# A fused attention and gated feed-forward block: scaling raw weight blocks on GpSimd, with a reordered start

## Chip, cores and metric

The kernel runs on one core of a Trainium2 chip. The metric is the device time of one execution in microseconds, the median of three runs.

## What is computed

One input `x` of 2048 tokens by 512 is normalised without weights. From it come a sliding-window attention with 32 heads of 16 and a window of 256, and a gated feed forward with 1792 inner columns. The result is `x` plus the product of both.

```python
xn = _layernorm(x)
# s: q, k, v = split(xn @ wqkv); softmax(q k^T / 4 inside the window) v; @ wo
s = _A_ref(xn, A_wqkv, A_wo)                 # H = 32, Dh = 16, W = 256
# B: (silu(xn @ w1) * (xn @ w3)) @ w2
g = _silu(_B_ref(xn, B_w1, B_w3, B_w2))      # F = 1792
return x + s * g
```

## The kernel before

All dense products run in three f16 terms: each f32 operand is scaled by a power of two and split in an upper half (`hi`, the f16 rounding) and a lower half (`lo`, the rest), and hi·hi, lo·hi and hi·lo are summed in PSUM. A split by `split` takes one ScalarE activation (hi, L215) and one VectorE instruction (lo, L216). The feed forward's weights are split by `split_pool`: ScalarE scales the raw block in place in f32 (L224), ScalarE casts it to f16 (L225), and GpSimd subtracts the one from the other in two halves of 256 columns (L221).

The scale of each block comes from its sum of squares. `measure(f)` takes two blocks f and f+1 of 128 feed-forward columns: six raw tiles are squared and summed (`squares`, four on ScalarE at L175, two on VectorE at L177), the sums are cast (`sb`, L187), TensorE multiplies them with ones (`ps`, L200), and a chain of small VectorE instructions makes the powers of two (`al`, `pp`, `pi`, L202 to L207 and L633 to L636). A step or two later the two blocks are split. `measure_down` does the same for the w2 blocks of a group of three or four.

Tokens go in four tiles of 512 (t), heads in four groups of eight (g), feed-forward columns in 14 blocks (f). The raw weights are loaded and split during t = 0 and the split blocks stored to DRAM (`dW1`, `dW2`), from where t = 1 to 3 load them. Raw blocks, split blocks and temporaries share 32 slots of 2 KB per partition (`take`, `give`), so an instruction that fills a slot waits for the last reader of the slot.

TensorE's instructions run in the order in which the Python code issues them; a scheduler orders the other engines. `later(n, f)` puts a function n steps on, and `step()` advances one step. After the start, work is cut into 32 units of attention. `batches` gives a unit's score and value matmuls (L474 for the maxima, L521 for the exponent, L549 for the values), and `spread` puts the dense pieces of six matmuls (L421 projections, L391 values, L682 gate and up, L727 down, L769 output) between those batches.

The start is written out by hand: load x and the first weights, `keep_busy` (filler matmuls that read only ones, L930), layer norm of tile 0 (L319 to L337), transposes on TensorE (L353) into two PSUM tiles `s` of two banks each, the split of the result (L356, L361), projections of group 0 and 1, and `value(0)`, `value(1)`. The softmax's row offsets enter the score product through two extra rows of the operands: `KA[0..2]` hold ones (times 4096) in rows 48, 49, 112 and 113. Before, a small tile `ones` is set by VectorE and six DMAs on SyncE's queue (L980) write it there.

Of the kernel before, what the change touches and what calls it, by code (L numbers as in the profile page):

```python
# [1 line left out]

# [6 lines left out]
F32 = mybir.dt.float32  # L9
BF16 = mybir.dt.bfloat16  # L10
F16 = mybir.dt.float16
# [8 lines left out]
P = 128  # L20
# [22 lines left out]
TERMS = 3  # L43
KR = TERMS * DH
ONE = 2.0**12
VW = DH + 1
VB = 10
SLOTS = 32
# [13 lines left out]
def tile_block(ctx: ExitStack, tc: tile.TileContext, x, wqkv, wo, w1, w3, w2, out):  # L62
# [26 lines left out]
    def take(dtype):  # L89
        slot = free.pop(0)  # L90
        made = fpool.tile([P, 512 if dtype == F32 else 1024], dtype, name=slot, tag=slot, bufs=1)
        held[id(made)] = slot, made
        return made

    def give(*tiles):
        for made in tiles:
            free.append(held.pop(id(made))[0])
# [14 lines left out]
    def later(n, f):  # L112
        made_so_far[0] += 1
        queue.append((now[0] + n, made_so_far[0], f))
# [93 lines left out]

    def scaled(a, by, name):
        t = const.tile([P, 1], F32, name=name)  # L210
        nc.vector.tensor_scalar(t, a, by, None, op0=ALU.mult)
        return t

    def split(hi, lo, raw, s):
# [6 lines left out]
            op(out[:, c], a[:, c], b[:, c])  # L221

    def split_pool(hi, lo, raw, s):
        nc.scalar.activation(raw, raw, AF.Copy, scale=s)  # L224
        nc.scalar.copy(hi, raw)  # L225
        halves(nc.gpsimd.tensor_sub, lo, raw, hi)


# [77 lines left out]
    def prepare(t):  # L306

        mv = lnpool.tile([P, 4, 2], F32, name="mv")
        rs = lnpool.tile([P, 4], F32, name="rs")
        xts = {}  # L310
        pair = {}

        def load(b):
            xts[b] = take(F32)
            (nc.scalar if t == 0 and b % 2 else nc.sync).dma_start(xts[b], x[t * TW + b * P:t * TW + (b + 1) * P, :])

        def stats(b):
            st = lnpool.tile([P, nc.vector.BN_STATS_DIM], F32, name="st")
            nc.vector.bn_stats(st, xts[b])  # L319
            nc.vector.bn_aggr(mv[:, b, :], st)  # L320

        def rstd(b0, b1):
            ve = lnpool.tile([P, b1 - b0], F32, name="ve")
            nc.vector.tensor_scalar(ve, mv[:, b0:b1, 1], 1e-5, None, op0=ALU.add)

            r0 = lnpool.tile([P, b1 - b0], F32, name="r0")
            nc.vector.tensor_scalar(r0.bitcast(I32), ve.bitcast(I32), 1, None, op0=ALU.logical_shift_right)
            nc.vector.tensor_scalar(r0.bitcast(I32), r0.bitcast(I32), -1.0, float(0x5F3759DF), op0=ALU.mult, op1=ALU.add)
            sq = lnpool.tile([P, b1 - b0], F32, name="sq")
            for i in range(3):  # L330
                nc.vector.tensor_mul(sq, r0, r0)
                nc.vector.scalar_tensor_tensor(sq, sq, -0.5, ve, op0=ALU.mult, op1=ALU.mult)
                nc.vector.scalar_tensor_tensor(r0, sq, 1.5, r0, op0=ALU.add, op1=ALU.mult)
            nc.vector.tensor_scalar(rs[:, b0:b1], r0, XS, None, op0=ALU.mult)

        def centre(b):
            lasts["centre"] = nc.vector.tensor_scalar(xts[b], xts[b], mv[:, b, 0:1], rs[:, b:b + 1],  # L337
                                                      op0=ALU.subtract, op1=ALU.mult)

        def turn(b):  # L340
            if t not in X:
                X[t] = xpool.tile([P, NC, TW], F16, name="XH"), xpool.tile([P, NC, TW], F16, name="XL")
            xh, xl = X[t]
            c = slice(b * P, (b + 1) * P)
            if t:
                pt = psm.tile([P, NC, P], F32, name="mm", tag="mm")
            else:

                if b % 2 == 0:
                    pair["s"] = pss.tile([P, 2, 512], F32, name="s")  # L350
                pt = pair["s"][:, b % 2, :].rearrange("p (k q) -> p k q", q=P)
            for k in range(NC):
                nc.tensor.transpose(pt[:, k, :], xts[b][:, k * P:(k + 1) * P], identf)  # L353
            give(xts.pop(b))
            with urgent():
                lasts["xh"] = nc.scalar.copy(xh[:, :, c], pt)  # L356

            def rest():
                turned[t] = turned.get(t, 0) + 1
                with urgent():  # L360
                    lasts["x"] = nc.vector.tensor_sub(xl[:, :, c], pt, xh[:, :, c])  # L361
            later(1, rest)
        return load, stats, rstd, centre, turn
# [82 lines left out]
    def fetch(t, g):  # L446
        QA[t, g] = qa = qpool.tile([P, 4, TW], F16, name="qa")
        ka = keys(t, g)
        c0 = 0 if t else 2 * P
        for dst, d in ((ka[:, :, c0:], dK[g][:, :, t * TW - 2 * P + c0:(t + 1) * TW]),  # L450
                       (qa, dQ[g][:, :, t * TW:(t + 1) * TW])):
            for r in range(2):
                nc.sync.dma_start(dst[64 * r:64 * r + KR],
                                  d[64 * r:64 * r + 64].rearrange("(a d) i t -> (d i) a t", d=DH))
# [348 lines left out]
    def feed_forward():  # L803

        pieces = []
        late = []
        for t in range(NT):
            for f in range(FB):
                if t == 0:
                    if f % 2:  # L810
                        pieces += [(0, lambda f=f: load(0, f)) for f in range(f + 3, min(f + 5, FB))]
                    elif f + 2 < FB:
                        pieces.append((0, lambda f=f + 2: measure(f, 1)))
                    pieces += [(0, lambda k=k: measure_down(k)) for k, (_, f1) in enumerate(GROUPS) if f == f1 - 1]
                else:
                    if f == 0:
                        pieces += [(0, lambda t=t, f=f: load(t, f)) for f in range(2)]
                    if f + 2 < FB:
                        pieces.append((0, lambda t=t, f=f + 2: load(t, f)))
                if f == FB - 4 and t + 2 < NT:  # L820
                    first, second = prepare_beside(t + 2)
                    pieces += first
                pieces += [(6, q) for q in gate_up(t, f)]
                pieces += late
                late = []
                for k, (f0, f1) in enumerate(GROUPS):
                    if f == f1 - 1:
                        late = [q for b in range(4) for q in down(t, k, b)]
            if t + 2 < NT:
                pieces += second  # L830
        return pieces + late
# [48 lines left out]
    def spread(made, dense):  # L880

        whole = sum(c for c, _ in dense) + sum(c for c, _ in made)
        dense = list(dense)
        at = 0
        for k, (cost, batch) in enumerate(made):
            batch()
            step()
            at += cost
            while dense and (at < whole * (k + 1) / len(made) or dense[0][0] == 0):
                c, piece = dense.pop(0)  # L890
                at += c
                piece()
                if c:
                    step()
        run(dense)

    def run(dense):
        for c, piece in dense:
            piece()
            if c:  # L900
                step()
# [3 lines left out]
    qk = [weights_qk(g) for g in range(NG)]  # L905
    wv = weights("wv", wqkv[:, 2 * D:3 * D])
    wout = weights("wo", wo)
    ones = take(F16)
    nc.vector.memset(ones[0:4, 0:KW], ONE)
    for b in range(4):  # L910
        load0(b)
    qk[0][0]()
    qk[1][0]()
    wv[0]()
# [7 lines left out]
    for b in range(VB):  # L922
        nc.gpsimd.memset(V[:, b, 0:H * VW].rearrange("p (h w) -> p h w", w=VW)[:, :, DH:VW], 1.0)
    nc.gpsimd.memset(V[:, :, H * VW:], 0.0)


    def keep_busy(n):
        ps = psm.tile([P, 4, P], F32, name="ps", tag="mm")
        for _ in range(n):
            nc.tensor.matmul(ps, onesb, onesb.unsqueeze(1).to_broadcast([P, 4, P]), start=True, stop=True)  # L930

    keep_busy(22)
    for b in range(4):
        stats0(b)
    qk[0][1]()
    qk[0][2]()
    keep_busy(9)
    rstd0(0, 4)
    for b in range(4):
        centre0(b)  # L940
# [10 lines left out]
        flush()  # L951
    with tc.issue_after(lasts["hi"].ins), tc.issue_after(lasts["x"].ins):
        qk[1][1]()
        wv[1]()
    keep_busy(4)


    k00, q00 = (project(0, 0, k, ((0,), (1,), (2,))) for k in (1, 0))
    run([k00[0], q00[0], k00[1], q00[1]])
    qk[1][2]()  # L960
    qk[1][3]()
    with tc.issue_after(lasts["hi"].ins):
        run([k00[2], q00[2]])
# [10 lines left out]
        measure(0)  # L974
    run(project(0, 1, 0))
    later(1, lambda: fetch(0, 1))
    run(value(0))
    for r in range(3):
        for q in range(2):
            nc.sync.dma_start(KA[r][64 * q + KR:64 * q + KR + 2], ones[2 * q:2 * q + 2, 0:KW].unsqueeze(1).to_broadcast([2, 4, KW]))  # L980
    give(ones)
    qk[2][1]()
    run(value(1))
    qk[2][2]()
# [91 lines left out]
```

## Time and profile before

| what | value |
|---|---|
| runs | 885.81, 888.51, 890.38 us; median 888.51 |
| profiled execution | 888.54 us, span 886.8 us |
| TensorE, weight load (PEld) | busy 847.0 us (96%), 375.9 us (42%) |
| VectorE (DVE) | 623.7 us (70%) |
| ScalarE (ACT) | 441.1 us (50%) |
| GpSimd (POOL) | 193.4 us (22%) |
| moved by DMA | 110.51 MB, 125 GB/s |

All times inside the execution are in microseconds from the start of the span. A row of the timeline gives start, duration, engine, line, operation, output and input tiles, and in brackets the idle time of the engine before it with what ended it. A name such as PEq or SPq is the engine's sequencer, where DMAs are issued. A group row gives count, total busy time and the mean in nanoseconds.

### The profile page before, as it was taken

The numbers are of one execution on the slowest core, as the hardware profiler recorded it, in microseconds if no ns is written. First come the engines' busy times: TensorE is split into PE (matmuls) and PEld (weight loads), VectorE is DVE, ScalarE is ACT, GpSimd is POOL, SyncE is SP. The second block draws the span as 40 slices with busy tenths as digits, with TensorE's granted clock in tenths as the row PEclk, the third lists the DMA queues.
The fourth block names the chain that finished last, engine by engine and source line by source line (L and its number), as shares of the span: only waits on it lengthen the run. The fifth ranks groups of instructions, "written<-read, shape, count | busy, mean of one in ns | idle before, by whom it ended". The sixth has DMA issues, their size and how long they took to land.

```text
span 886.8 us, 20443 instructions
## 1 busy us (share of the span) xinstructions
PE 847.0 (96%) x7814; PEld 375.9 (42%) x7814; DVE 623.7 (70%) x1833; ACT 441.1 (50%) x649; POOL 193.4 (22%) x308
## 2 busy tenths in 40 slices
PE   7968898999999999999999999999999999999997
PEld 3323344344444444444444444444444444444443
DVE  7676866797678667768767776777767786666435
ACT  4777767673435544443444444444444444444521
POOL 1236226352111202111111112120211103131211
PEclk9989999999999999999999999999999999999999
DMA  9864525646543343452445333533443353332201
GB/s 294 222 221 157 154 80 170 182 147 192 149 133 95 103 118 111 108 150 73 125 121 128 100 89 103 160 102 101 117 126 79 87 140 111 99 110 84 75 9 60
DMA packets 95133, 110.51 MB, mean 125 GB/s; under 512 B 16972, under 2 KB 60348, under 8 KB 95036
## 3 DMA queue, kind: packets, MB, share of 16 engines
q1 hardware_dynamic: 94748, 108.69, 42.9%
q8 instruction: 61, 1.00, 0.5%
q10 hardware_dynamic: 288, 0.52, 0.2%
q14 instruction: 36, 0.29, 0.1%
HBM read 76.28 MB, written 28.57 MB: 118 GB/s over the span
## 4 chain that ended last, share of the span: by engine, by line
PE 70%; DVE 9%; ACT 6%; DMA 5%; issue 5%; POOL 3%; SPq 1%; POOLq 0%; DVEq 0%; ACTq 0%
PE mm L682 25%; PE mm L727 14%; PE po L549 8%; PE mm L421 6%; PE s L521 6%; PE s L474 4%; PE mm L769 4%; PE mm L391 3%; DVE junk L479 3%; POOL slot L221 2%; DMA slot<-in_A_x_dram 1%; ACT pt L539 1%; DMA slot<-in_B_w_dram 1%; ACT sqa L175 1%; ACT slot L225 1%
## 5 line engine op out<-in xcount | busy, mean ns | idle before, releaser
L539 ACT ACTIVATE pt<-s,es 128x1024 f32<-128x1024 f32 (+1 forms) x184 | 200.9, 1094 | 224.0 <-DVE s L535 115.3
L682 PE MATMUL mm<-XH,slot 128*128 128x512 f16 x896 | 269.2, 382 | 1.6 <-DVE XL L361 1.2
L221 POOL TENSOR_TENSOR slot<-slot,slot 128x256 f16<-128x256 f32 (+1 forms) x220 | 146.9, 694 | 537.5 <-ACT slot L706 410.3
L479 DVE CUSTOM_DVE_ANT_0 junk<-s,MW 128x320 bf16<-128x320 f32 x448 | 218.0, 487 | 24.0 <-PE s L474 13.7
L682 PEld LDWEIGHTS <-slot 128*128 128x128 f16 x1344 | 121.7, 98 | 161.7 <-issue 29.4
L682 PE MATMUL mm<-XL,slot 128*128 128x512 f16 x448 | 170.5, 381 | 0.0
L727 PE MATMUL mm<-slot,slot 128*128 128x512 f16 x672 | 160.7, 383 | 1.7 <-DVE XL L361 1.4
L535 DVE TENSOR_TENSOR s<-s,M 128x512 f32<-128x512 f32 x128 | 89.0, 696 | 72.4 <-PE s L521 67.6
L549 PE MATMUL po<-pt,V 128*32 128x128 f32 (+1 forms) x1920 | 98.3, 330 | 0.0
L727 PEld LDWEIGHTS <-slot 128*128 128x128 f16 x672 | 61.1, 98 | 82.6 <-issue 16.3
L474 PE MATMUL s<-KA,qa 48*64 48x320 f16 (+2 forms) x1024 | 73.6, 298 | 12.6 <-DVE M L479 8.5
L530 DVE TENSOR_TENSOR s<-s,M 128x1024 f32<-128x1024 f32 x56 | 68.8, 1228 | 19.6 <-PE s L521 15.9
L521 PE MATMUL s<-qa,KA 50*64 50x128 f16 (+1 forms) x1920 | 74.2, 251 | 5.6 <-ACT pt L539 2.8
L521 PEld LDWEIGHTS <-KA 50*64 50x64 f16 x1920 | 33.7, 105 | 80.2 <-issue 47.4
L697 DVE SCALAR_TENSOR_TENSOR slot<-slot,mm 128x512 f32<-128x512 f32 x56 | 38.4, 685 | 41.3 <-ACT slot L693 41.1
L706 ACT CAST slot<-slot 128x512 f16<-128x512 f32 x56 | 34.5, 616 | 53.2 <-DVE slot L702 53.1
L549 PEld LDWEIGHTS po<-pt,V 128*32 128x32 f32 x1920 | 49.8, 109 | 24.8 <-issue 12.0
L693 ACT ACTIVATE slot<-mm,sgs 128x512 f32<-128x512 f32 x56 | 38.2, 682 | 27.5 <-PE mm L682 23.8
L702 DVE SCALAR_TENSOR_TENSOR slot<-mm,slot 128x512 f32<-128x512 f32 x56 | 38.6, 688 | 18.6 <-PE mm L682 18.5
L221 POOL TENSOR_TENSOR on<-on,rb 128x256 f32<-128x256 f32 x32 | 22.6, 727 | 127.9 <-DMA qa<-dm 82.9
L743 DVE SCALAR_TENSOR_TENSOR slot<-mm,dsc,slot 128x512 f32<-128x512 f32 x48 | 35.9, 749 | 20.5 <-PE mm L727 20.4
L421 PE MATMUL mm<-XH,whi 128*128 128x512 f16 x128 | 47.1, 381 | 1.2 <-ACT whi L215 1.2
(122 smaller groups left out, 828.1 us busy)
## 6 DMA issues: line engine op xcount, KB each, us to landing
slot<-dW SPq DMA_DIRECT2D x126, 256.0 KB
slot<-in_B_w_dram SPq DMA_DIRECT2D x42, 256.0 KB
dW<-slot SPq DMA_DIRECT2D x42, 256.0 KB
slot<-in_A_x_dram SPq DMA_DIRECT2D x30, 256.0 KB
KA<-dK SPq DMA_DIRECT2D x24, 288.0 KB
qa<-dQ SPq DMA_DIRECT2D x32, 192.0 KB
dK<-slot SPq DMA_DIRECT2D x16, 256.0 KB
dQ<-slot SPq DMA_DIRECT2D x16, 256.0 KB
```

The costliest lines, as they stand in the source:

```text
L221: op(out[:, c], a[:, c], b[:, c])
L421: nc.tensor.matmul(cell["pp"], a[:, k, c, :], b[:, c, :], start=(c, i) == parts[0][0], stop=(c, i) == parts[-1][-1])
L474: nc.tensor.matmul(s[64 * c:64 * c + 64, r, :n], qa[rows, 2 * p + a, ii * P + 64 * c:ii * P + 64 * c + 64], ka[rows, 2 * p + a, e - n:e], ...
L479: nc.vector.tensor_tensor_reduce(out=junk[:, :n], in0=s[:, r, :n], in1=mask, scale=1.0, scalar=NEG, op0=ALU.add, op1=ALU.max, accum_out=M[ ...
L521: nc.tensor.matmul(s[h:h + 64, r, o:o + w * P], ka[rows, 2 * p + a, (j + 2) * P + h:(j + 2) * P + h + 64], qa[rows, 2 * p + a, q * P:(q + ...
L530: nc.vector.tensor_add(sv, sv, m.unsqueeze(1).to_broadcast([P, 4, 2, P]))
L535: nc.vector.tensor_add(sv[:, :, b, :], sv[:, :, b, :], M2[:, k:k + 1, :].to_broadcast([P, 4, P]))
L539: nc.scalar.activation(pt[:, :, 0:n], s.rearrange("p r (a q) -> p (r a) q", a=2)[:, :, 0:n], AF.Exp, scale=es)
L549: nc.tensor.matmul(cell["po"][32 * i:32 * i + 32, q * P:(q + w) * P], V[:, (4 * t + j) % VB, h * VW:h * VW + 32], pt[:, i, o:o + w * P], s ...
L682: nc.tensor.matmul(cell[k], w[:, (a * NC + c) * P:(a * NC + c + 1) * P], b[:, c, :], start=c == 0 and i == 0, stop=c == NC - 1 and i == 2)
L702: nc.vector.scalar_tensor_tensor(sg, cell[1], 0.5 * HS / (WS * XS)**2, sg, op0=ALU.mult, op1=ALU.mult)
L727: nc.tensor.matmul(ps, hh[:, a * TW + b * P:a * TW + (b + 1) * P], w[:, c * D:(c + 1) * D], start=f == f0 and i == 0, stop=f == f1 - 1 and ...
```

## The change

Six things are changed together.

- `split_pool`: ScalarE writes hi straight from the raw block with the scale; GpSimd multiplies the raw block by the scale in place, in two halves, and then subtracts as before.
- The rows of ones: no DMA any more. VectorE sets all of `KA[0]`, ScalarE all of `KA[1]` from a tile of ones, GpSimd all of `KA[2]`.
- Transposes of tile 0: each of the four has its own PSUM tile (two `s`, one `po`, one `mm`).
- The fillers: 27, 5 and 4 where there were 22, 9 and 4.
- `wv`'s squares come after the scale of `qk[1]`, whose product stands four matmuls earlier; `measure(2, 1)` is called before `value(0)`, and not at block 0 of the feed forward.
- `spread`: after each batch, dense pieces are issued as long as at least half of the next one lies within the share of dense work due by then; before, as long as that share was not yet reached.

```diff
+TWO_ONES = struct.unpack("f", struct.pack("ee", ONE, ONE))[0]
...
     def split_pool(hi, lo, raw, s):
-        nc.scalar.activation(raw, raw, AF.Copy, scale=s)
-        nc.scalar.copy(hi, raw)
+        nc.scalar.activation(hi, raw, AF.Copy, scale=s)
+        for c in (slice(0, 256), slice(256, 512)):
+            nc.gpsimd.tensor_scalar(raw[:, c], raw[:, c], s, None, op0=ALU.mult)
         halves(nc.gpsimd.tensor_sub, lo, raw, hi)
...
-            if t:
+            if t or b == 3:
                 pt = psm.tile([P, NC, P], F32, name="mm", tag="mm")
+            elif b == 2:
+                pt = pso.tile([P, TW], F32, name="po").rearrange("p (k q) -> p k q", q=P)
             else:
-                if b % 2 == 0:
-                    pair["s"] = pss.tile([P, 2, 512], F32, name="s")
-                pt = pair["s"][:, b % 2, :].rearrange("p (k q) -> p k q", q=P)
+                pt = pss.tile([P, 2, 512], F32, name="s")[:, 0, :].rearrange("p (k q) -> p k q", q=P)
...
-                    elif f + 2 < FB:
+                    elif 0 < f < FB - 2:
                         pieces.append((0, lambda f=f + 2: measure(f, 1)))
...
-            while dense and (at < whole * (k + 1) / len(made) or dense[0][0] == 0):
+            while dense and (at + dense[0][0] / 2 <= whole * (k + 1) / len(made) or dense[0][0] == 0):
...
-    ones = take(F16)
-    nc.vector.memset(ones[0:4, 0:KW], ONE)
     for b in range(4):
         load0(b)
+    nc.vector.memset(KA[0].rearrange("p a c -> p (a c)").bitcast(F32), TWO_ONES)
+    nc.scalar.activation(KA[1].rearrange("p a (b c) -> p (a b) c", c=P), onesb.unsqueeze(1).to_broadcast([P, 24, P]),
+                         AF.Copy, scale=ONE)
...
+    for a in range(4):
+        nc.gpsimd.memset(KA[2][:, a, :].bitcast(F32), TWO_ONES)
...
-    keep_busy(22)
+    keep_busy(27)
...
-    keep_busy(9)
+    keep_busy(5)
...
         qk[1][1]()
-        wv[1]()
     keep_busy(4)
     k00, q00 = (project(0, 0, k, ((0,), (1,), (2,))) for k in (1, 0))
-    run([k00[0], q00[0], k00[1], q00[1]])
+    run([k00[0], q00[0], k00[1]])
     qk[1][2]()
+    with tc.issue_after(lasts["scale"].ins):
+        wv[1]()
+    run([q00[1]])
     qk[1][3]()
...
     later(1, lambda: fetch(0, 1))
+    measure(2, 1)
     run(value(0))
-    for r in range(3):
-        for q in range(2):
-            nc.sync.dma_start(KA[r][64 * q + KR:64 * q + KR + 2], ones[2 * q:2 * q + 2, 0:KW].unsqueeze(1).to_broadcast([2, 4, KW]))
-    give(ones)
```

More of the change, by code (lines that the diff above doesn't have):

```diff
@@ L1 @@
+import struct
 from contextlib import ExitStack, nullcontext
```

3 lines of the change are left out of this document (1 added, 2 removed).

## The prediction

> **What bounds the kernel now.** I read the page first, then busy time by stage, then TensorE's waits, then the timeline of the stage with the longest wait.
>
> ```profile
> span 886.8 us, 20443 instructions
> PE 847.0 (96%) x7814; PEld 375.9 (42%) x7814; DVE 623.7 (70%) x1833; ACT 441.1 (50%) x649; POOL 193.4 (22%) x308
> ```
> ```profile
> 0.00:60.00 60.00, 47.83 (x247) 20.91 (x248) 42.02 (x162) 38.33 (x84) 14.22 (x40) 0.94 0.83 239
> 60.00:200.00 140.00, 125.84 (x1090) 55.02 (x1089) 105.07 (x377) 98.94 (x175) 62.34 (x96) 0.99 0.51 155
> 200.00:860.00 660.00, 651.30 (x6371) 289.62 (x6370) 463.48 (x1274) 299.54 (x384) 112.08 (x168) 1.00 0.40 111
> 860.00:886.80 26.80, 22.06 (x111) 10.35 (x109) 13.10 (x21) 4.33 (x7) 4.78 (x8) 0.98 0.16 50
> ```
> ```profile
> PE s L474 <- DVE M L479: 8.5, 10, 2.0
> PE ps L200 <- DVE sb L187: 7.4, 3, 5.3
> ```
>
> The columns of the second fence are stretch, length, then busy time of PE, PEld, DVE, ACT and POOL, then TensorE's granted clock, DMA share and GB/s. TensorE is the bound: busy 847.0 of 886.8 us. It idles 60 - 47.83 = 12.2 us in the first 60 us, 14.2 us from 60 to 200, 8.7 us in the next 660 and 4.7 at the end. The matmuls that compute stay the same, so the change can only move idle time, filler matmuls, and time at a lower clock; all three lie mostly in front. After 200 us hardly anything is left to win. The third fence (engine line, who it waited for: total, times, longest) shows that one wait of 5.3 us stands out.
>
> ```profile
> 45.67 0.60 PE L682 MATMUL mm<-XH,slot 128*128 128x512 f16 x2
> ```
> ```profile
> 46.32 0.59 PE L682 MATMUL mm<-XH,slot 128*128 128x512 f16 x2
> ```
> ```profile
> 48.41 0.63 ACT L175 ACTIVATE sqa<-slot 128x512 bf16<-128x512 f32 x1
> ```
> ```profile
> 52.22 0.17 DVE L187 CAST sb<-ssq 128x6 bf16<-128x6 f32 x1 [1.97 <-ACT sqa L175]
> 52.45 0.17 PE L200 MATMUL ps<-sb,onesb 128*128 128x6 bf16 x1 [5.32 <-DVE sb L187]
> 52.55 0.75 PE L474 MATMUL s<-KA,qa 48*64 48x320 f16 x8
> ```
> ```profile
> 53.23 1.04 PE L682 MATMUL mm<-XH,slot 128*128 128x512 f16 x2
> ```
> ```profile
> 57.31 0.31 PE L474 MATMUL s<-KA,qa 48*64 48x128 f16 x8
> ```
>
> This is `measure(2)`: TensorE's order is written by hand, so its small L200 product blocks all behind it until the squares of blocks 2 and 3 are summed, and ScalarE starts those only at 48.41. After the stall the same pair of matmuls that took 0.59 us takes 1.04: the clock has fallen.
>
> **The change part by part.**
>
> *measure(2) is moved ahead of `value(0)`.* In the built kernel its L200 now stands some 60 matmuls earlier, before `value(2)`, and the score matmuls follow block 0's feed forward directly. Gone: 5.3 us of stall. Gone too: the slow stretch behind it. From 52.55 to 57.31 there are 8 score matmuls and 12 of L682 in 4.76 us; at the early pace (a pair and its single from 45.67 to 46.32, three matmuls in 0.65 us, so 12 in 2.6) plus 0.75 they take 3.3. That is 1.4 us. The granted clock of 0.94 over the first 60 us holds this stretch. The Trainium skill ("TensorE: Matmul & The Clock Gate", Part 1) says that an idle window of about 3.4 us halves TensorE's clock until a busy window has passed; the pair's 1.04 against 0.59 us agrees. Together 5.3 + 1.4 = 6.7 us.
>
> *What the moved squares now stand in front of.* This is the debit, and it hangs on ScalarE's queue.
>
> ```profile
> 12.55 1.09 PE L353 MATMUL s<-identf,slot 128*128 128x128 f32 x8 [0.68 <-ACT XH L356]
> 14.37 0.66 PE L353 MATMUL s<-identf,slot 128*128 128x128 f32 x4 [0.73 <-ACT XH L356]
> 21.39 0.15 DVE L211 TENSOR_SCALAR sw<-invqk 128x1 f32<-128x1 f32 x1
> ```
> ```profile
> 22.35 1.04 PE L421 MATMUL mm<-XH,whi 128*128 128x512 f16 x4 [1.24 <-ACT whi L215]
> 25.62 0.15 DVE L211 TENSOR_SCALAR swwv<-invwv 128x1 f32<-128x1 f32 x1
> ```
> ```profile
> L177 DVE CUSTOM_DVE_ANT_0 sqd<-slot 128x512 bf16<-128x512 f32 x20 | 14.2, 725 | 5.8 <-DMA slot<-in_B_w_dram 5.6
> ```
> ```profile
> 30.95 0.57 ACT L430 ACTIVATE slot<-mm 128x512 f16<-128x512 f32 x1
> 31.30 0.17 PE L200 MATMUL ps<-sb,onesb 128*128 128x6 bf16 x1 [0.60 <-DVE sb L187]
> 32.00 0.62 ACT L175 ACTIVATE sqa<-slot 128x512 bf16<-128x512 f32 x1
> 34.31 0.19 PE L200 MATMUL ps<-sb,onesb 128*128 128x1 bf16 x2
> 40.31 0.59 PE L682 MATMUL mm<-XH,slot 128*128 128x512 f16 x2
> ```
>
> First the start. One filler matmul more in all stands where TensorE waits anyway: 0. With a PSUM bank for each transpose the waits of 0.68 and 0.73 go, 1.4 us. With `wv`'s squares behind the scale of `qk[1]` the wait of 1.24 goes. But what is late next is `swwv` (25.62). The scale of `qk[1]` (21.39) comes to about 18.3: 1.4 earlier by the start, and some 1.7 by squares that stood before it. From there VectorE's new order has nine instructions on 128x512 before `swwv` (four squares at 0.725, the two cuts and three L434, which I price alike at 0.7) and a few small ones: 18.3 + 6.4 + 0.2 = 24.9. So it is 0.7 to 0.9 us earlier, not 2.6, and TensorE then waits about 1 us for `wvh`. So ScalarE reaches L430 (30.95) at about 30.1 and TensorE its L200 (31.30) at 30.4.
>
> From there ScalarE's new order is: L430 and the evacuation of V (30.95 to 32.00, 1.05 us), four squares of `measure(2)` and two of `qk[2]`, at 0.61 us each. That is 30.1 + 1.05 + 3.7 = 34.9. TensorE's L200 for `qk[2]` (34.31, without a wait) needs the last of them: it moves to 35.1, 0.8 later than before, after a wait of about 1.7. A further 0.4 goes to the product of `measure(2)` itself and the bank it frees. Block 0's first matmul goes from 40.31 to about 41.5. Net of the whole start: +1.2 us. The bounds are -2.6 (the start's gain kept whole) and +2.5 (the waits of 1 to 1.7 us also drop the clock once more).
>
> *The rows of ones.*
>
> ```profile
> 1.55 0.70 DVE L909 MEMSET slot<- 4x768 f16 x1
> ```
> ```profile
> 6.77 0.63 ACT L175 ACTIVATE sqa<-slot 128x512 bf16<-128x512 f32 x1 [3.82 <-DMA slot<-in_A_wqkv_dram]
> ```
> ```profile
> L539 ACT ACTIVATE pt<-s,es 128x1024 f32<-128x1024 f32 x176 | 195.5, 1112 | 218.2 <-DVE s L535 109.5 <-DVE s L530 107.7 <-ACT slot L706 0.3
> ```
> ```profile
> L539 ACT ACTIVATE pt<-s,es 128x512 f32<-128x512 f32 x8 | 5.4, 681 | 5.8 <-DVE s L535 5.8
> ```
> ```profile
> 35.64 2.64 SPq L980 DMA_DIRECT2D KA<-slot  x4
> ```
>
> VectorE's memset grows from 768 to 1536 elements, so from 0.70 to about 1.4, and ends at 3.0, when it waits for x. ScalarE fills 3072 elements before its first square; at 0.43 us for 512 more (0.681 for 512, 1.112 for 1024) that is some 2.8 us, inside the 3.82 that it waits. GpSimd's four memsets lie where it has nothing to do. SyncE loses six issues, 2.64 us of them in front of the next loads; but behind those stands the store of block 0's weights, which waits for GpSimd, so I give no credit. Nothing here reaches TensorE: 0. If the cover of VectorE or ScalarE failed it would cost what sticks out, under 1 us.
>
> *The split of the raw blocks.*
>
> ```profile
> L225 ACT CAST slot<-slot 128x512 f16<-128x512 f32 x42 | 24.6, 612 | 4.7 <-POOL slot L221 3.0 <-DMA dK<-slot 1.7
> ```
> ```profile
> L215 ACT ACTIVATE whi<-slot,sw 128x512 f16<-128x512 f32 x8 | 5.5, 717 | 5.5 <-DVE sw L211 5.5
> ```
> ```profile
> L221 POOL TENSOR_TENSOR slot<-slot,slot 128x256 f16<-128x256 f32 x196 | 130.0, 690 | 494.5 <-ACT slot L706 410.3 <-ACT slot L225 82.3 <-issue 1.4
> ```
> ```profile
> masks.py:199 POOL TENSOR_SCALAR_AFFINE_SELECT identf<-identf 128x128 f32<-128x128 f32 x1 | 0.3, 293 | 0.0
> ```
> ```profile
> 82.98 0.39 PE L682 MATMUL mm<-XH,slot 128*128 128x512 f16 x1 [0.36 <-POOL slot L221]
> ```
>
> ScalarE loses 42 casts, 24.6 us; the scaling that is left writes f16, as L215's does, at 0.717 each. GpSimd gains 84 multiplies. No such instruction is in the trace: the one-input select on half the elements (0.293) and the two-input subtraction of the same size (0.690) are the ends. I take 0.45, nearer the one-input row, with part of it fixed and the elements doubled: 38 us, range 25 to 58. By the Trainium skill ("GPSIMD Engine Reference", § 3.1) a tight one-input loop takes about 1.8 cycles an element, an estimate of 0.38 us for 256, so 32 us. GpSimd is busy 62 of 140 us between 60 and 200; with three quarters of the new work there it comes to about 90. The lower half is ready after one activation, two multiplies and two subtractions, 0.7 + 0.9 + 1.4 = 3.0 us; before, two activations and the same subtractions, 2.7 us. The one place where TensorE waited for it (0.36) stays about that. On SyncE's in-order queue the loads of block 6 now stand behind the stores of blocks 1 and 2, which wait for GpSimd's halves; the squares that need those loads come some 20 us later, so 0. ScalarE's relief and GpSimd's load I set against each other: 0, from -3 to +4.
>
> *Piece spreading.* `spread` now rounds to the nearest piece rather than up. In the built order the runs of dense matmuls between attention batches shift by one piece; before 78 runs of 6, 66 of 12, 44 of 18, after 72, 72, 41. No work is added; at stake are the waits left after 60 us, 14.2 + 8.7 = 23 us. I take 0, plus or minus 4.
>
> *Sum.* -6.7 + 1.2 = -5.5. The profiled execution took 888.54 us with a span of 886.8, 1.7 outside it; the runs' median is 888.51, so both give the same: 883.0 us, -0.6%. What a measurement of this kernel can tell from no change is about 0.5%, 4.4 us.
>
> **The rivals.**
>
> *The front gains whole and the later waits shrink too (chance 0.20).* The start keeps its 2.6 us, and of the 23 us some 4 go, ScalarE being 24.6 us lighter. For: TensorE also waits for ScalarE between 60 and 200. Against: VectorE's waits are larger. 888.5 - 6.7 - 2.6 - 4 = 875.
>
> *The stall only moves (0.17).* The waits of 1 and 1.7 us around 30 to 35 grow to a long one, since six squares stand in a row before `qk[2]`'s product, and the clock falls there: +2.5 and 1.4 more than my sum. 888.5 - 5.5 + 3.9 = 887. For: ScalarE's queue stands between all the steps there. Against: 1 and 1.7 us are well under the 5.3 that the slow matmuls followed.
>
> *GpSimd takes VectorE's port, and VectorE's lateness reaches TensorE: slower (0.18).*
>
> ```profile
> 53.06 0.17 DVE L206 TENSOR_SCALAR pp<-al 128x6 f32<-128x6 f32 x1
> ```
> ```profile
> 77.97 1.30 POOL L221 TENSOR_TENSOR slot<-slot,slot 128x256 f16<-128x256 f32 x2 [1.57 <-ACT slot L706]
> 78.70 0.59 DVE L206 TENSOR_SCALAR pp<-al 128x6 f32<-128x6 f32 x1
> ```
>
> The same 6-element instruction takes 0.17 us with GpSimd idle and 0.59 during one of its subtractions. If each of the 84 multiplies holds up VectorE by 0.42 us, that is 35 us; where 40% of it reaches TensorE through the scores' maxima (the 8.5 us line above), 14 us: 888.5 - 5.5 + 14 = 897. Against: the slow row reads and writes SBUF alone, while the maxima and mask additions read PSUM. It decides once more than 10 us reach TensorE. The Trainium skill has this rule ("GPSIMD Engine Reference", § 8): GpSimd shares its SBUF interfaces with VectorE, and § 4.1 prefers VectorE for elementwise work. By that rule the time is this rival's; the rows agree on a small instruction, and no run here shows a multiply.
>
> **How the numbers follow.** The forecast has 0.45 and its own range 878 to 888. Chances: forecast 0.45, of which 0.33 lies below 884.1 and 0.12 within 0.5%; first rival 0.20, faster; second 0.17, of which 0.02 faster and 0.15 same; third 0.18, slower. So faster 0.55, same 0.27, slower 0.18. The range for 8 in 10 takes in the forecast, the second rival and most of the first, and the lower part of the third: 874 to 892.
>
> **What would show each step.** Right: no wait above 2.1 us before an L200 behind block 0, a granted clock near 1.0 from 50 to 60, block 0's first matmul at 41 to 42, the L474 now at 57.31 at about 52; GpSimd's busy time at 218 to 253 and ScalarE's at about 419. Wrong: a wait of over 2.1 us before `qk[2]`'s product, TensorE's idle time from 60 to 200 well off 14, L206-like rows of 0.6 us in most blocks, or multiplies above 0.69 us.

## The result and the profile after

The changed kernel takes 936.35 us (median of four runs, 935.12 to 938.62) against 887.32 us (885.81 to 890.38) for the kernel before: a ratio of 1.0566, 95% interval 1.0542 to 1.0590. That is slower by 49 us. The forecast was 883.0 us, range 874 to 892. The profiled execution took 938.62 us with a span of 936.8.

From the page of the changed kernel, the span and the busy times:

```profile
span 936.8 us, 20492 instructions
...
PE 866.8 (93%) x7815; PEld 382.0 (41%) x7815; DVE 632.4 (68%) x1833; ACT 423.1 (45%) x608; POOL 270.0 (29%) x396
```

Busy time by stage, in the columns of the prediction's second fence:

```profile
0.00:60.00 60.00, 51.42 (x274) 22.76 (x275) 43.97 (x170) 39.24 (x83) 30.29 (x61) 1.00 0.87 242
60.00:200.00 140.00, 101.30 (x712) 41.63 (x711) 79.00 (x258) 57.55 (x100) 88.97 (x119) 0.81 0.34 105
200.00:860.00 660.00, 642.06 (x6280) 283.92 (x6278) 474.03 (x1351) 301.81 (x395) 138.69 (x200) 0.99 0.42 117
```

The first 60 us became better: TensorE is busy 51.42 us where it was 47.83, at a clock of 1.00 where it was 0.94. The next 140 us lost it all. TensorE is idle 140 - 101.3 = 38.7 us there (14.2 before) and runs at a granted clock of 0.81 (0.99). Over the whole span idle time went from 886.8 - 847.0 = 39.8 to 936.8 - 866.8 = 70.0 us, 30 more; busy time grew by 20 us for practically the same matmuls. So of the 50 us, three fifths are waiting and two fifths are matmuls that ran slower. Five waits of TensorE between 60 and 200 us last 6.6, 3.8, 4.1, 7.1 and 8.3 us (they end at 97.72, 117.08, 127.19, 163.16 and 196.09), 29.9 of the 38.7; in the 4 us behind each of them the granted clock is 0.50. Before, no wait of TensorE in this stage was longer than 2.0 us.

GpSimd's groups by line, operation and shape:

```profile
L224 POOL TENSOR_TENSOR slot<-slot,slot 128x256 f16<-128x256 f32 x196 | 128.3, 677 | 399.1 <-ACT slot L709 399.1
L229 POOL TENSOR_SCALAR slot<-slot,pi 128x256 f32<-128x256 f32 x56 | 53.1, 959 | 42.1 <-ACT slot L227 42.1
L229 POOL TENSOR_SCALAR slot<-slot,sw 128x256 f32<-128x256 f32 x28 | 25.9, 937 | 28.6 <-ACT slot L227 28.6
```

L229 is the new multiply, L224 the subtraction (L221 before). A multiply takes 0.94 to 0.96 us, not 0.45, and more than a subtraction that reads two inputs. One block occupies GpSimd for 2 x 0.95 + 2 x 0.68 = 3.26 us where it took 2 x 0.69 = 1.38.

How that reaches TensorE is seen in the list of waits (who, for whom: total, times, longest):

```profile
PE s L477 <- DVE M L482: 26.2, 9, 8.2
...
ACT slot L227 <- POOL slot L224: 23.6, 5, 7.7
ACT sqa L178 <- DMA slot<-in_B_w_dram: 23.5, 8, 8.6
...
ACT O L596 <- POOL on L224: 17.6, 6, 10.3
...
PE s L524 <- ACT pt L542: 10.6, 7, 6.3
...
PEld L685 <- POOL slot L229: 7.3, 1, 7.3
PE mm L685 <- DVE slot L700: 7.1, 1, 7.1
```

The three waits of ScalarE in the kernel before:

```profile
ACT O L593 <- POOL on L221: 13.4, 8, 2.8
...
ACT sqa L175 <- DMA slot<-in_B_w_dram: 3.3, 3, 1.9
...
ACT slot L225 <- POOL slot L221: 3.0, 4, 1.5
```

TensorE's matmuls wait for VectorE's maxima (L482) and for ScalarE's exponents (L542), hardly ever for GpSimd itself. One weight load (PEld) is put down to GpSimd with 7.3 us; it starts 0.01 us after the matmul in front of it, and that matmul's wait is the last line of the list. But ScalarE waits for GpSimd, and other engines wait for ScalarE. The longest wait of TensorE, in the timeline; the rows between the lines shown are left out:

```profile
189.31 1.83 POOL L229 TENSOR_SCALAR slot<-slot,pi 128x256 f32<-128x256 f32 x2
191.09 1.30 POOL L224 TENSOR_TENSOR slot<-slot,slot 128x256 f16<-128x256 f32 x2
192.34 1.41 POOL L224 TENSOR_TENSOR on<-on,rb 128x256 f32<-128x256 f32 x2
193.79 0.62 ACT L596 CAST O<-on 128x512 f16<-128x512 f32 x1 [10.28 <-POOL on L224]
194.31 0.59 ACT L433 ACTIVATE slot<-mm 128x512 f16<-128x512 f32 x1
...
194.94 0.69 DVE L437 SCALAR_TENSOR_TENSOR slot<-mm,slot 128x512 f16<-128x512 f32 x1 [8.64 <-ACT slot L433]
...
195.54 0.48 DVE L482 CUSTOM_DVE_ANT_0 junk<-s,MW 128x320 bf16<-128x320 f32 x1
...
196.09 0.32 PE L477 MATMUL s<-KA,qa 48*64 48x128 f16 x4 [8.25 <-DVE M L482]
```

GpSimd works through weight blocks without a pause until 192.34 and only then normalises the attention's output (`on`). ScalarE's next instruction, the cast of it, has stood 10.28 us at the head of its queue. Behind the cast stands L433, behind that VectorE's L437 (8.64 us), behind that the maxima, and TensorE has waited 8.25 us. No one on that chain needs a weight block. The maker of the delay is GpSimd's order, and the engine that TensorE's row names is three links further.

A second way goes through SyncE's queue (SPq), to the wait of 6.6 us:

```profile
90.33 3.38 SPq L690 DMA_DIRECT2D dW<-slot  x2
...
92.06 1.29 POOL L224 TENSOR_TENSOR slot<-slot,slot 128x256 f16<-128x256 f32 x2
...
93.80 0.38 SPq L318 DMA_DIRECT2D slot<-in_A_x_dram  x1
...
96.64 0.69 DVE L322 BATCH_NORM_STATS2 st<-slot 128x6 f32<-128x512 f32 x1 [7.31 <-DMA slot<-in_A_x_dram]
...
97.72 0.43 PE L477 MATMUL s<-KA,qa 48*64 48x256 f16 x4 [6.59 <-DVE M L482]
```

The store of a split block (L690) stands at the head of SyncE's queue until GpSimd has made the lower half at 93.35; the load of x behind it goes out at 93.80, VectorE's statistics stand 7.31 us for it, and TensorE 6.59.

A third way goes through the slots, to the wait of 7.1 us:

```profile
158.21 0.72 ACT L227 ACTIVATE slot<-slot,sw 128x512 f16<-128x512 f32 x1 [6.18 <-POOL slot L224]
...
161.71 0.69 ACT L696 ACTIVATE slot<-mm,sgs 128x512 f32<-128x512 f32 x1 [2.17 <-POOL slot L224]
...
162.43 0.69 DVE L700 SCALAR_TENSOR_TENSOR slot<-slot,mm 128x512 f32<-128x512 f32 x1 [3.69 <-ACT slot L696]
...
163.16 1.01 PE L685 MATMUL mm<-XH,slot 128*128 128x512 f16 x2 [7.06 <-DVE slot L700]
```

ScalarE stands twice until a subtraction on GpSimd lets it write a slot, VectorE stands for ScalarE, and TensorE for the PSUM bank that VectorE reads. How the loss divides among the three ways is not measured.

### The profile page after: what moved, and what is told of

Same layout as the page of the kernel before. It is cut to its first block, busy times and chain, and to the rows that moved or that the text cites. A ratio compares the mean times of both kernels' runs of the same rounds, so it can differ in the third digit from the quotient of the medians.

```text
span 936.8 us, 20492 instructions
## 1 busy us (share of the span) xinstructions
PE 866.8 (93%) x7815; PEld 382.0 (41%) x7815; DVE 632.4 (68%) x1833; ACT 423.1 (45%) x608; POOL 270.0 (29%) x396
## 4 chain that ended last, share of the span: by engine, by line
PE 67%; POOL 12%; issue 8%; DVE 6%; ACT 4%; DMA 3%; SPq 0%; POOLq 0%; ACTq 0%; DVEq 0%
PE mm L685 23%; PE mm L730 12%; PE po L552 8%; POOL slot L229 6%; PE mm L424 5%; PE s L524 5%; POOL slot L224 5%; PE mm L772 4%; PE mm L394 4%; PE s L477 3%; DVE s L533 2%; DVE junk L482 2%; ACT pt L542 1%; PE ps L937 1%; DMA slot<-in_B_w_dram 1%
## 5 line engine op out<-in xcount | busy, mean ns | idle before, releaser
L542 ACT ACTIVATE pt<-s,es 128x1024 f32<-128x1024 f32 (+1 forms) x184 | 200.8, 1093 | 209.2 <-DVE s L533 104.3
L685 PE MATMUL mm<-XH,slot 128*128 128x512 f16 x896 | 275.7, 390 | 9.1 <-DVE slot L700 7.1
L224 POOL TENSOR_TENSOR slot<-slot,slot 128x256 f16<-128x256 f32 (+1 forms) x220 | 145.2, 682 | 441.1 <-ACT slot L709 399.1
L482 DVE CUSTOM_DVE_ANT_0 junk<-s,MW 128x320 bf16<-128x320 f32 x448 | 217.9, 486 | 31.8 <-PE s L477 21.0
L685 PEld LDWEIGHTS <-slot 128*128 128x128 f16 x1344 | 124.1, 100 | 175.2 <-issue 38.3
L685 PE MATMUL mm<-XL,slot 128*128 128x512 f16 x448 | 173.7, 388 | 0.0
L730 PE MATMUL mm<-slot,slot 128*128 128x512 f16 x672 | 164.8, 391 | 0.3
L730 PEld LDWEIGHTS <-slot 128*128 128x128 f16 x672 | 62.3, 100 | 83.2 <-issue 18.0
L229 POOL TENSOR_SCALAR slot<-slot,pi 128x256 f32<-128x256 f32 x56 | 53.1, 959 | 42.1 <-ACT slot L227 42.1
L224 POOL TENSOR_TENSOR on<-on,rb 128x256 f32<-128x256 f32 x32 | 22.6, 727 | 127.7 <-DMA qa<-dm 65.4
L477 PEld LDWEIGHTS <-qa 48*64 48x64 f16 x1024 | 29.0, 107 | 57.4 <-DVE M L482 30.4
```

The costliest lines, as they stand in the source:

```text
L229: nc.gpsimd.tensor_scalar(raw[:, c], raw[:, c], s, None, op0=ALU.mult)
L477: nc.tensor.matmul(s[64 * c:64 * c + 64, r, :n], qa[rows, 2 * p + a, ii * P + 64 * c:ii * P + 64 * c + 64], ka[rows, 2 * p + a, e - n:e], ...
L482: nc.vector.tensor_tensor_reduce(out=junk[:, :n], in0=s[:, r, :n], in1=mask, scale=1.0, scalar=NEG, op0=ALU.add, op1=ALU.max, accum_out=M[ ...
L542: nc.scalar.activation(pt[:, :, 0:n], s.rearrange("p r (a q) -> p (r a) q", a=2)[:, :, 0:n], AF.Exp, scale=es)
L685: nc.tensor.matmul(cell[k], w[:, (a * NC + c) * P:(a * NC + c + 1) * P], b[:, c, :], start=c == 0 and i == 0, stop=c == NC - 1 and i == 2)
L730: nc.tensor.matmul(ps, hh[:, a * TW + b * P:a * TW + (b + 1) * P], w[:, c * D:(c + 1) * D], start=f == f0 and i == 0, stop=f == f1 - 1 and ...
```

## The experiments

Three theories of the loss stood at first. Theory 1: the multiplies make GpSimd the slow stage while t = 0, and queues that run in order stall behind it. Theory 2: each multiply takes a port from VectorE, and VectorE is late. Theory 3: the loss is in the start or the spreading. The kernel before ran beside every group, at medians of 886.5 to 887.9 us, so comparisons across groups go by ratio to it; differences of ratios are turned into us with 887.3.

### Which part loses

`rest_only`: the changed kernel with the old split.

```diff
-        nc.scalar.activation(hi, raw, AF.Copy, scale=s)
-        for c in (slice(0, 256), slice(256, 512)):
-            nc.gpsimd.tensor_scalar(raw[:, c], raw[:, c], s, None, op0=ALU.mult)
+        nc.scalar.activation(raw, raw, AF.Copy, scale=s)
+        nc.scalar.copy(hi, raw)
         halves(nc.gpsimd.tensor_sub, lo, raw, hi)
```

> The changed kernel with the old split of the raw blocks (two ScalarE instructions, GpSimd only subtracts); start, measure(2), rows of ones and spreading stay changed. Theory 1 (the multiplies make GpSimd the slow stage of the weight preparation while t = 0, and engines that run in order stall behind it): all the loss is gone and the front's gain is left, 888.5 - 5.5 = 883 us, 880 to 886, GpSimd busy about 196 us, no wait above 3 us on TensorE between 60 and 200 us. Theory 2 (the multiplies slow VectorE through a shared port): the same 883. Theory 3 (the new order of the start or of the dense pieces loses): over 900 us.

Measured: 883.13 us, ratio 0.9959 (0.9944 to 0.9974). `split_only` is the kernel before with the opposite edit, the new split alone:

> The kernel before with only the split of the raw blocks changed. Theories 1 and 2: the loss as a whole, 936.4 + 5.5 = 942 us, 930 to 948, with GpSimd busy about 272 us and TensorE idle some 35 to 40 us between 60 and 200 us. Theory 3: under 900 us.

Measured: 934.24 us, ratio 1.0530 (1.0507 to 1.0553). So the loss is the split, Theory 3 falls as its cause, and the other parts together gain 0.4%. On top of them the split costs 1.0566 - 0.9959 = 0.0607, 54 us; on the kernel before 0.053, 47 us. In `rest_only` the stage after the first 60 us and the wait for the normalised output (L595 there is L596 above) are:

```profile
60.00:200.00 140.00, 127.94 (x1112) 56.21 (x1109) 106.24 (x377) 92.10 (x158) 62.21 (x96) 0.99 0.49 149
```
```profile
ACT O L595 <- POOL on L224: 9.7, 7, 2.3
```

TensorE's idle time is 12.1 us in place of 38.7, and the longest wait of that kind 2.3 us in place of 10.3.

### Is it the length of GpSimd's work?

`pool_tt_mul`: the same product as a multiply of two tensors.

```diff
-            nc.gpsimd.tensor_scalar(raw[:, c], raw[:, c], s, None, op0=ALU.mult)
+            nc.gpsimd.tensor_mul(raw[:, c], raw[:, c], s.to_broadcast([P, 256]))
```

> The changed kernel with the in-place multiply written as a product of two tensors (the scale's column repeated along the row) in the same two halves. If GpSimd's cost goes by the number of inputs that it reads with a step, it takes 0.67 us as the subtraction does, 84 x 0.28 = 23 us less on GpSimd; by Theory 1 the loss of some 54 us (936.4 - 882) then falls to between a third and three quarters, 900 to 923 us. If a repeated column is as slow as the scalar (0.93 us or more), the time stays at 936 or grows. Theory 2 (number of GpSimd instructions that VectorE meets): about 936 as well.

Measured: 912.91 us, ratio 1.0294 (1.0268 to 1.0320).

```profile
L229 POOL TENSOR_TENSOR slot<-slot,pi 128x256 f32<-128x256 f32 x56 | 34.6, 639 | 41.7 <-ACT slot L227 41.7
...
L229 POOL TENSOR_TENSOR slot<-slot,sw 128x256 f32<-128x256 f32 x28 | 17.0, 627 | 29.3 <-ACT slot L227 29.3
```

The multiply takes 0.63 us, and the loss over `rest_only` falls from 54 to 30 us. With as many instructions but 27.4 us less of GpSimd's time, 24 us of the loss went: this part goes by length and not by number. Whether the 30 us that remain go by length alone was not tried. The same kernel also shows that multiplies shorter than the prediction's upper bound, 0.69 us, cost about 30 us, not 0 to 4.

`pool_whole` (one multiply of 512 columns) and `pool_imm` (a constant in place of the scale's column, so its blocks are not rightly scaled) price the instruction:

```diff
-        for c in (slice(0, 256), slice(256, 512)):
-            nc.gpsimd.tensor_scalar(raw[:, c], raw[:, c], s, None, op0=ALU.mult)
+        nc.gpsimd.tensor_scalar(raw, raw, s, None, op0=ALU.mult)
```
```diff
-            nc.gpsimd.tensor_scalar(raw[:, c], raw[:, c], s, None, op0=ALU.mult)
+            nc.gpsimd.tensor_scalar(raw[:, c], raw[:, c], 64.0, None, op0=ALU.mult)
```

> The changed kernel with one multiply of 512 columns on GpSimd in place of two of 256. If an instruction has a large fixed part: 1.2 to 1.5 us for the 512 and 915 to 925 us in all; if its price goes by elements: 1.8 to 1.9 us and 936.

> The changed kernel with the multiply by a constant in place of the block's scale (its product is then not the scaled block), to price the instruction: if the scale's column makes it slow, 0.3 to 0.5 us a multiply and 890 to 905 us in all; if the one-input form itself does, 0.92 us and 936 us.

Measured, one run each: 931.10 us (`pool_whole`) and 929.81 us (`pool_imm`).

```profile
L228 POOL TENSOR_SCALAR slot<-slot,pi 128x512 f32<-128x512 f32 x28 | 44.3, 1587 | 40.5 <-ACT slot L227 40.5
```
```profile
L229 POOL TENSOR_SCALAR slot<-slot 128x256 f32<-128x256 f32 x84 | 71.6, 868 | 68.9 <-ACT slot L227 68.9
```

512 columns take 1.59 us, between the two expectations, and 256 take 0.95: some 0.3 us fixed and 0.64 for 256 elements. A constant saves only 0.09, near the second expectation. It is the form with one tensor and one scalar that is dear here.

### Port, latency or queue?

`idle_multiplies`: the old split, and 84 such multiplies where GpSimd has time, in t = 1 to 3.

```diff
...
                     halves(nc.gpsimd.tensor_sub, hh[:, TW:], sg, hh[:, 0:TW])
+                    if t:
+                        for c in (slice(0, 256), slice(256, 512)):
+                            nc.gpsimd.tensor_scalar(sg[:, c], sg[:, c], sg_scale[:, f:f + 1], None, op0=ALU.mult)
                     give(sg)
```

> The changed kernel with the old split of the raw blocks (883.1 us), and 84 GpSimd multiplies of the same shape put where GpSimd has time, in the feed forward of t = 1 to 3, two behind each lower half of a product, on the dead product. (Their result is not used.) Theory 1 (only GpSimd's queue in t = 0 matters): 883, 880 to 887. Theory 2 (each multiply holds up VectorE by 0.42 us and 40% reaches TensorE): +14, 897 us; if a multiply of 0.93 us holds VectorE up for as long as it runs, +31, 914 us. VectorE's rows on 128x512 would then be longer than in the kernel without them.

Measured: 885.75 us, ratio 0.9987 (0.9974 to 1.0000), 2.5 us over `rest_only`, whose interval it just touches. GpSimd was busy with them nearly as long as in the changed kernel (79.0 us):

```profile
L712 POOL TENSOR_SCALAR slot<-slot,sgs 128x256 f32<-128x256 f32 x84 | 77.0, 929 | 0.0
```

VectorE's small instructions on SBUF do get longer. `rest_only`, then `idle_multiplies`, the same line:

```profile
L487 DVE SCALAR_TENSOR_TENSOR nm<-M,nm 128x16 f16<-128x16 f32 x32 | 6.3, 198 | 0.8
```
```profile
L487 DVE SCALAR_TENSOR_TENSOR nm<-M,nm 128x16 f16<-128x16 f32 x32 | 8.0, 249 | 0.8
```

That is the contention which Theory 2 builds on, and in this stage it is worth some 2.5 us, not 14 to 31. In the changed kernel itself, where the multiplies stand in t = 0, the same instruction (L488 there) has a mean of 204 ns and the squares on VectorE, L180, 831 (749 in `rest_only`); VectorE's whole busy time is 6.8 us above that of `rest_only`, far less than the 54 us. Theory 2 falls as the main cause; that a few of the 54 us come this way is not excluded.

`late_multiplies`: the old split, and the multiplies behind the subtractions, on the dead raw block.

```diff
-        nc.scalar.activation(hi, raw, AF.Copy, scale=s)
+        nc.scalar.activation(raw, raw, AF.Copy, scale=s)
+        nc.scalar.copy(hi, raw)
+        halves(nc.gpsimd.tensor_sub, lo, raw, hi)
         for c in (slice(0, 256), slice(256, 512)):
             nc.gpsimd.tensor_scalar(raw[:, c], raw[:, c], s, None, op0=ALU.mult)
-        halves(nc.gpsimd.tensor_sub, lo, raw, hi)
```

> The changed kernel with the old split of the raw blocks, and then the 84 GpSimd multiplies behind the subtractions of each block, on the raw block that nobody reads any more: GpSimd has the same work and a raw slot is held as long, but a block's own lower half doesn't wait for its multiplies. (The multiplies' result is not used.) If it is GpSimd's queue (each block occupies it for 3.2 us, and the next blocks queue behind that): 920 to 936 us, as the changed kernel. If it is the way of one block (two multiplies more before its lower half): near 883 us, at most 895. Slots alone (raw blocks given back later): also 920 or more, but with ScalarE's squares waiting for loads and no waits for lower halves.

Measured: 927.74 us, ratio 1.0462 (1.0435 to 1.0490), 45 us over `rest_only`. So some 45 of the 54 us come without any block's lower half waiting for its own multiplies: the loss is in what comes behind them. That is the later work in GpSimd's queue, and whoever needs the raw slot that a multiply still holds. The second is seen too; L231 is the multiply:

```profile
ACT slot L228 <- POOL slot L231: 13.8, 4, 5.5
```

`scratch_multiplies` was meant to tell the two apart: its multiplies are on a scratch tile, for which one of the 32 slots had to go. `slots31` is its base, without multiplies.

```diff
-SLOTS = 32
+SLOTS = 31
...
+    scratch = const.tile([P, 256], F32, name="scratch")
...
-        nc.scalar.activation(hi, raw, AF.Copy, scale=s)
+        nc.scalar.activation(raw, raw, AF.Copy, scale=s)
+        nc.scalar.copy(hi, raw)
+        halves(nc.gpsimd.tensor_sub, lo, raw, hi)
         for c in (slice(0, 256), slice(256, 512)):
-            nc.gpsimd.tensor_scalar(raw[:, c], raw[:, c], s, None, op0=ALU.mult)
-        halves(nc.gpsimd.tensor_sub, lo, raw, hi)
+            nc.gpsimd.tensor_scalar(scratch[:, 0:256], scratch[:, 0:256], s, None, op0=ALU.mult)
```

> The old split of the raw blocks in the changed kernel, and behind each block's subtractions two GpSimd multiplies on a scratch tile of its own (one slot less in the pool to make room): GpSimd has the same work, but neither a lower half nor a raw slot waits for a multiply of its own block. (The scratch is not used.) GpSimd's queue (later blocks wait behind the multiplies): 915 to 930 us, as with the multiplies on the dead raw block (927.7). Raw slots held longer, and so loads late: near 883, at most 893.

> The changed kernel with the old split and one slot less in the pool (31), with no multiplies on GpSimd: the base against which the multiplies on a scratch tile (949.1) have to be read. If the missing slot costs little: 883 to 888 us, and the scratch multiplies cost 61 to 66 us by GpSimd's queue alone. If slots are short: 900 us or more, and the scratch run says that much less about the queue.

Measured: 949.14 us, ratio 1.0684 (1.0667 to 1.0702), and 888.38 us, ratio 1.0014 (0.9996 to 1.0033). The missing slot costs 5 us, and the multiplies on scratch 0.067 more, 59 us. Neither expectation was met, and the trace shows why the run doesn't separate the two: the built order is not the order of the code. These multiplies read only the block's scale, so the scheduler put many of them ahead of the subtractions. At 31.99 eight run in a row, before the first subtraction at 40.00, and GpSimd stood idle for them until VectorE's chain for the scales was done; later TensorE waits for GpSimd directly:

```profile
POOL scratch L234 <- DVE p L643: 40.2, 4, 26.4
...
PE mm L689 <- POOL slot L227: 9.1, 3, 4.9
```

So lower halves do wait for multiplies here, and a raw slot is held until its late subtraction. What the run shows is that 84 multiplies which touch no raw block cost as much, through the place that they take in GpSimd's order. How much of the 54 us is later work in GpSimd's queue and how much is raw slots held longer stays open.

### The work taken from GpSimd

`lower_on_vector`: VectorE makes the lower half in one instruction.

```diff
         nc.scalar.activation(hi, raw, AF.Copy, scale=s)
-        for c in (slice(0, 256), slice(256, 512)):
-            nc.gpsimd.tensor_scalar(raw[:, c], raw[:, c], s, None, op0=ALU.mult)
-        halves(nc.gpsimd.tensor_sub, lo, raw, hi)
+        nc.vector.scalar_tensor_tensor(lo, raw, s, hi, op0=ALU.mult, op1=ALU.subtract)
```

> The changed kernel, with the lower half of a raw block made by one VectorE instruction (raw times scale minus upper half, as the split of the projection weights does), so GpSimd has no part in the blocks. VectorE gets 42 x 0.75 = 31.5 us, nearly all before 200 us, where it is busy about 147 of 200 us. Theory 1: the long waits for GpSimd go, 883 us as without the new split, 878 to 890, or a few us less by ScalarE's 24.6 us. If instead every step added to an engine in t = 0 reaches TensorE in part (40% of 31.5): 895 us. Theory 2 says less than 890 too, since GpSimd is idle.

Measured: 876.91 us, ratio 0.9883 (0.9864 to 0.9902), 6.7 us under `rest_only`.

```profile
L228 DVE SCALAR_TENSOR_TENSOR slot<-slot,pi,slot 128x512 f16<-128x512 f32 x28 | 21.0, 756 | 0.0
```
```profile
60.00:200.00 140.00, 130.94 (x1143) 57.51 (x1141) 124.71 (x413) 79.62 (x129) 23.64 (x30) 0.99 0.50 150
```

VectorE is busy 124.7 of 140 us, fuller than GpSimd (89) was in the changed kernel, and TensorE waits 9.1 us there, less than in any kernel above. A busy share does not tell which engine delays; who stands behind whom does. GpSimd lost the subtractions of the blocks as well as the multiplies here, and ScalarE 42 casts; which of the two gives the 6.7 us is not separated. The Trainium skill ("GPSIMD Engine Reference", § 4.1) puts elementwise work on VectorE rather than GpSimd; these runs agree, 0.76 us for the whole lower half against 3.26. The same row calls one-input work on GpSimd roughly line rate; the 0.95 us against 0.68 for the two-input subtraction do not agree with that.

### The other parts

`move_only` and `spread_only` are the kernel before with one edit each; `no_spread` is the changed kernel with the old split and the old rounding, so start, move and rows of ones.

```diff
-                    elif f + 2 < FB:
+                    elif 0 < f < FB - 2:
...
+    measure(2, 1)
     run(value(0))
```
```diff
-            while dense and (at < whole * (k + 1) / len(made) or dense[0][0] == 0):
+            while dense and (at + dense[0][0] / 2 <= whole * (k + 1) / len(made) or dense[0][0] == 0):
```

> The kernel before with measure(2) alone moved ahead of value(0). The prediction's term: 6.7 us for the stall and the slow matmuls behind it, less 0.8 to 1.2 us that the six moved squares cost in front: 886.5 - 5.7 = 880.8 us, 878 to 883. If the stall only moves to the product of qk[2]: 885 to 888.

> The kernel before with only the rounding in spread changed. The prediction's term was 0, plus or minus 4 us: 886.5. The start, the move and the spreading together gave -3.4 us where the start and the move had been put at -5.5; if the spreading is what takes the rest away, +2 us here, 888.5; if it is what gives the gain, 883.

> The changed kernel with the old split and the old rounding in spread: what is left is the start, the move of measure(2) and the rows of ones. By the prediction's term for the start (+1.2) on the move alone as measured (0.9926): 882 us. By the difference of the runs (0.9959 / 1.0063 / 0.9926 = 0.997, -2.7 us for the start): 878 us.

Measured: `move_only` 880.28 us, 0.9926 (0.9906 to 0.9945); `spread_only` 892.96 us, 1.0063 (1.0039 to 1.0088); `no_spread` 878.19 us, 0.9891 (0.9876 to 0.9906). The move is worth 6.6 us. The start with the rows of ones is worth 0.9926 - 0.9891, 3.1 us, with intervals that just touch. The spreading loses 5.6 us alone and 0.9959 - 0.9891, 6.0 us, on the other parts. With its cost alone the sum is -6.6 - 3.1 + 5.6 = -4.1, and `rest_only` has -3.6, so the parts nearly add up.

Block 0's first matmul (40.31 before) in `move_only`, then in `no_spread`:

```profile
42.34 0.60 PE L682 MATMUL mm<-XH,slot 128*128 128x512 f16 x2
```
```profile
40.16 0.59 PE L684 MATMUL mm<-XH,slot 128*128 128x512 f16 x2
```

The moved squares cost 2.0 us in front, and the start gives 2.2 of them back. Part of the spreading's loss is seen from 80 to 100 us, in `no_spread` and then in `rest_only`:

```profile
80.00:100.00 20.00, 17.34 (x135) 7.12 (x134) 17.42 (x72) 13.83 (x26) 7.41 (x12) 1.00 0.55 166
```
```profile
80.00:100.00 20.00, 15.42 (x117) 6.14 (x117) 16.20 (x62) 12.03 (x21) 8.34 (x14) 0.91 0.48 150
```

TensorE is idle 4.6 us in place of 2.7, and its clock falls to 0.91. Why the shifted pieces make just these waits was not tried.

`best` joins what won: the changed kernel with the lower half on VectorE (as above) and the old rounding.

> The changed kernel with the lower half of the raw blocks made by one VectorE instruction and with the old rounding in spread; start, move and rows of ones stay changed. The lower half on VectorE gave a ratio of 0.9883 with the new rounding, and the new rounding alone 1.0063. If the two simply add: 0.9883 / 1.0063 = 0.982, 871.5 us, 869 to 874. If the new rounding only costs where GpSimd's or ScalarE's work for the blocks is late: 877 us, as with the new rounding.

Measured: 874.46 us, ratio 0.9850 (0.9835 to 0.9864): 1.5% faster than the kernel before and 6.8% than the changed one (0.9850 / 1.0566). The gain of the old rounding is 2.9 us here, between the two expectations: with the lower half on VectorE the rounding costs about half of its 6.0 us. Whether GpSimd's relief or ScalarE's takes the other half was not tried.

## Why the prediction was wrong

**What failed: the split, priced at 0 (-3 to +4); it cost 54 us on top of the other parts and 47 on the kernel before.** Two steps failed one after the other.

*The multiply's price.* The estimate was 0.45 us between a select (0.293 on half the elements) and the subtraction (0.690); the chip showed 0.95. The two-input row was taken as the upper end for an operation with one tensor. That is no bound for another operation: the trace of before had no multiply by a scalar on GpSimd, and nothing in it excluded more. The prediction did name multiplies above 0.69 us as a sign of being wrong. GpSimd's busy time came to 270 us, above the 218 to 253 named. The Trainium skill's 1.8 cycles an element, a best case ("GPSIMD Engine Reference", § 3.1), gives an estimate of 0.38 us for 256 elements and was further off than the row; the measured time decides.

*Setting load off against relief.* Even with the right price the term was built wrongly. At 0.63 us a multiply (`pool_tt_mul`), below the prediction's own bound of 0.69, the split costs 30 us, not 4. "ScalarE's relief and GpSimd's load I set against each other" weighed busy times of two engines, neither of which bounded the stage. From 60 to 200 us GpSimd was busy 89 us, as the prediction said (about 90), and that is luck, since each multiply cost twice the estimate and more of them fell outside the stage; the loss came all the same. What counts is who stands behind the blocks in GpSimd's order: the attention's `on` and `O`, the slots that ScalarE writes next and the stores ahead of SyncE's loads. The prediction named the waiter it saw (0.36 us of TensorE for a lower half) and that wait indeed stayed small, 0.2 us; the ones that grew were ScalarE's for GpSimd, 10.3 us at the longest (2.8 before). The prediction shows such a wait, 3.0 us in L225's row, and makes nothing of it. "The squares that need those loads come some 20 us later, so 0" failed in the same way: ScalarE's squares waited 23.5 us for loads (3.3 before).

**What was right, and by how much.** The stall of 5.3 us is gone and the clock from 50 to 60 us is 1.00. The move gave 6.6 us in all, where 6.7 less some of the debit was forecast. The debit's place was right: the wait before `qk[2]`'s product is 1.55 us, forecast 1.7, and none before an L203 is longer. The start was mis-sized: +1.2 forecast with its debit, while block 0's first matmul came at 40.13 instead of 41.5. With the debit of 2.0 (`move_only`) the start gives 2.2 there and 3.1 in the whole time, close to the 2.6 of the bound. The score matmuls that stood at 57.31 come at 49.26 and 51.40, forecast 52. The rows of ones showed no cost: ScalarE's fill took 2.76 us, forecast 2.8, and ended 1.04 us before its first square.

**The spreading** lay outside its bound of 4: +5.6 alone, +6.0 with the rest. Without the split the forecast's sum of -5.5 would have met -3.6, a near number by luck: the front gave -9.7 (`no_spread`) where -5.5 was forecast, and the spreading took 6.0 of it back.

**The rivals.** The third rival had the sign and the engine right, GpSimd, but by its port: 14 us through VectorE. `idle_multiplies` puts the port at 2.5 us, in another stage. A rival in which GpSimd's longer queue holds up ScalarE was missing. The first rival's terms for the front did hold: -6.7 - 2.6 = -9.3, against -9.7 in `no_spread`.

## What to carry to other kernels

When work moves to an engine off the critical path, list what else stands in that engine's queue and who waits for it; price the longer queue through those, stage by stage, and never against another engine's relief. An instruction that the trace does not show has no upper bound from a row of another operation; leave the range open above it, or measure the instruction. In a list of waits, follow the named releaser back until it is an engine that is working, not one that is waiting too.

## What the runs showed of the hardware

A GpSimd multiply of a tensor by a scalar took 0.95 us for 128x256 f32 (1.59 for 128x512), longer than a subtraction or product of two tensors of 128x256 (0.68 and 0.63); repeating the scalar's column as a second tensor saved a third. After each of five waits of 3.8 to 8.3 us TensorE's granted clock was 0.50 for the next 4 us; from 60 to 200 us it was 0.81 on average, and TensorE's busy time grew by 20 us for as many matmuls.
